# Forty weight columns instead of 64 in three groups of products, and PSUM pairs as three fixed tiles, in a chunked RWKV-7 kernel with a feed-forward block

## The chip, the cores and the metric

The kernel runs on one core of a Trainium2 chip. The core has five engines, each with its own queue of instructions: PE (matrix products; its weight loads are shown as PEld), DVE (vector work), ACT (activations and copies), POOL (vector work without access to PSUM) and SP (here it issues transfers). The metric is the device time of one execution in microseconds (us), lower is better; times are given as the median of several runs. All data are 32-bit floats. A matmul of this type that is no transpose shows as two weight loads and two matmul records in the profile, so the record counts below are twice the program's matmuls, except for transposes.

PSUM, where PE writes, has eight banks; a bank is 128 partitions by 512 floats.

## The reference

```python
# r, k, v, w, a, b: (batch 4, heads 8, time 768, D 40)
state = zeros((B, H, D, D))
for t in range(S):
    y[:, :, t] = einsum('bhd,bhde->bhe', rt, state)
    Sa = einsum('bhde,bhe->bhd', state, at)
    state_decay = state * wt[:, :, None, :] - einsum('bhd,bhe->bhde', Sa, bt)
    state = state_decay + einsum('bhd,bhe->bhde', vt, kt)

# x: y with (heads, D) as features, 3072 tokens x 320
h = x @ w_in                                   # 320 -> 2048
g = h * clip(h + 3.0, 0.0, 6.0) / 6.0
out = g @ w_out                                # 2048 -> 320
```

## The kernel before, in words

The recurrence is done in blocks of 64 time steps. A unit is one block of two batches with all eight heads; 24 units, four to a group of 128 steps (two blocks by two pairs of batches). For each unit, preparation stages (function `prepare`) load and transpose the inputs, form running products of the decays on DVE (scans, L541 and L552), and the score products; an inversion of a triangular matrix for a whole group runs on DVE as a long row of small steps (`invert`, L738 and L744), with its second half on PE (`third_block`, L773 and L796). The unit's own stages (function `step`) then follow: R (L853), U (L891), U-transpose (L911), the product with the state before the block (rS, L927), the new state (sn, L946, its addition on DVE at L954), scores (H, C, from `scores`, L509) and y (L969). ACT copies most of these results out of PSUM (U L895, U-transpose L917, rS L933, S L880, EV L692); POOL multiplies y by the decay and SP moves it into the layout of the feed-forward block.

The products of a block are small: D is 40, a block 64 steps. The kernel uses the PE array in quarters of 64 rows by 64 columns, and four matmuls, one to a quarter, work side by side. In y, U-transpose and rS the weights are slices of 64 columns (`SLOT`) although a head has 40; the other 24 columns produce rows of the result that nobody reads. The new state's products (L946) load 64 columns in the first four units and 40 (`D`) in the rest.

The feed-forward block works on 128 tokens, one unit, in two jobs of eight feature tiles each. A job has an `expand` (L1051: 24 matmuls, 48 records, into two banks called the hidden ones, half `c` = 0 and 1, 512 columns each) and a `contract` (L1092: eight matmuls, 16 records, into a bank called `o`). Between them, for each half in turn, ACT takes the relu out of the hidden bank (L1066) and DVE forms the product with the same bank (L1067) into `gt`. The function `results` issues them in the order relu 0, product 0, relu 1, product 1. The contract of one job is issued after the expand of the next. 48 jobs in all. Jobs are dealt out between the unit stages by `pieces`, a matmul group at a time.

The order of instructions on every engine is the order in which the Python code issues them. Semaphore waits come from a layer that follows who wrote and read each tile; two uses of one tile by different engines are put in order where they touch.

PSUM: one bank `one`, one bank `o`, and three pairs of banks. A call to `pair()` gives the next pair, of which the two banks hold what the two row halves of the array write. Before, two of the pairs are slots of a pool (`pair`, two buffers) and the third is in a pool of its own (`lent`). The three are called in turn. When the feed-forward block begins (`begun_ffn`), the `lent` pool is closed and a pool for two hidden banks takes its place; from then on `pair()` asks the pool with two slots. Such a pool gives a new tile the slot whose last use comes first in the order of issue, and a tile's first writer waits for every user of the slot's last tile.

Of the kernel before, what the change touches and what calls it, by code (L numbers as in the profile page):

```python
# [8 lines left out]
F32 = mybir.dt.float32  # L9
# [3 lines left out]
AF = mybir.ActivationFunctionType  # L13
AX = mybir.AxisListType
PSUM = bass.MemoryType.PSUM

P = 128
# [3 lines left out]
SLOT = 64  # L21
# [3 lines left out]
def _ap(ap, extra, dims):  # L25

    return bass.AP(tensor=ap.tensor, offset=ap.offset + extra, ap=[list(ap.ap[0])] + dims)
# [3 lines left out]
def kernel(  # L31
# [42 lines left out]
    nc = tc.nc  # L74
    B, H, T, D = r.shape
# [17 lines left out]
    ps = ctx.enter_context(tc.tile_pool(name="ps", bufs=1, space=PSUM))  # L93
# [3 lines left out]
        return ps.tile(shape, F32, name=tag, tag=tag, bufs=bufs)  # L97

    ring, open_half = deque(), [None]
    lent = tc.tile_pool(name="lent", bufs=1, space=PSUM)  # L100
    pools = {"lent": lent.__enter__(), "pair": ps}
    pairs = deque([("pair", 2), ("pair", 2), ("lent", 1)])

    def pair():

        pairs.rotate(-1)
        tag, bufs = pairs[-1]
        return pools[tag].tile([P, 2, 512], F32, name=tag, tag=tag, bufs=bufs)

    def begun_ffn():  # L110

        lent.__exit__(None, None, None)
        pairs.clear()
        pairs.append(("pair", 2))
        pools["h"] = ctx.enter_context(tc.tile_pool(name="hidden", bufs=1, space=PSUM))


    def ps_any(shape):
# [21 lines left out]
    def ps_pair(*dims):  # L140

        n = 1
        for d in dims:
            n *= d
        if shared[0] is None or shared[1] + n > 512:
            shared[:] = pair(), 0
            open_half[0] = None
        at = shared[1]
        shared[1] += n
        views, step = [], n  # L150
        for d in dims:
            step //= d
            views.append([step, d])
        t = shared[0][:]
        return [_ap(t, at, views), _ap(t, at + 512, views), _ap(t, at, [[512, 2]] + views)]
# [6 lines left out]
        out=ident[:], in_=ones, pattern=[[1, P]],  # L162
# [4 lines left out]
        out=ones[:, 0:BL], in_=ones[:, 0:BL], pattern=[[1, BL]],  # L167
# [3 lines left out]
        out=ones[BL:P, 0:BL], in_=ones[BL:P, BL:P], pattern=[[1, BL]],  # L171
# [5 lines left out]
    three = const.tile([P, 1], F32, name="three")  # L177
# [43 lines left out]
    for i in range(3):  # L221
        t = const.tile([P, H, BL], F32, name=f"score{i}")
# [7 lines left out]
    RR = const.tile([P, 2, NPR * D + SLOT - D], F32, name="RR")  # L230
# [6 lines left out]
    for p in range(NP):  # L237
        t = const.tile([P, 2, NPR, SLOT], F32, name=f"state{p}")
        nc.vector.memset(t[:], 0.0)
        state.append(t)  # L240
        t = const.tile([P, 2, NPR], F32, name=f"last{p}")
# [16 lines left out]
    for i, (x, y) in enumerate([(0, DFF // 2), (0, NJ // 2)]):  # L258
        for n, z in enumerate((x, y)):
            t = win[:, :, z:z + H * SLOT] if i == 0 else \  # L260
                wout[:, z:z + 4, :].rearrange("p j m -> p (j m)")[:, 0:2 * H * SLOT].rearrange(
                    "p (n x) -> p n x", n=2)
            t = t.rearrange("p n (h e) -> p n h e", e=SLOT)
            name = ("WA", "BK")[i][n]
# [3 lines left out]
    for u in range(2):  # L268
        t = win2[:, u * NPR * P:(u + 1) * NPR * P]
# [216 lines left out]
    def by_banks(x):  # L486
        return x[:].rearrange("p r (q t) -> p q r t", q=2)
# [8 lines left out]
    def turned(name):  # L496
        return tmp.tile([P, NPR, P], F32, name=name, tag="turned", bufs=5)

    def half(i, n=SLOT):
        return slice(SLOT * i, SLOT * i + n)  # L500
# [316 lines left out]
    def step(i):  # L817

        n, o = i % NU, data[i]
        g, p = names[i]  # L820
# [3 lines left out]
        m = {}  # L824
# [78 lines left out]
        def s_UT():  # L903

            up = ps_pair(2, P)
            for j in range(2):
                for s in range(2):
                    for x in range(2):
                        for rs in range(2):
                            pr = 2 * j + rs  # L910
                            nc.tensor.matmul(out=up[x][half(rs), j, half(x ^ s)],  # L911
                                             lhsT=RR[half(x), s, pr * D:pr * D + SLOT],
                                             rhs=tinv[half(x), n * H + 4 * s + pr, :],
                                             start=True, stop=True)
            yield PE
            m["UT"] = turned("UT")
            nc.scalar.activation(out=m["UT"][:].rearrange("p (x j) t -> p x j t", x=2), in_=up[2],  # L917
                                 func=AF.Copy, scale=-1.0)

        def s_rS():  # L920

            ysp = ps_pair(2, 2, BL)
            for j in range(2):
                for q in range(2):
                    for s in range(2):
                        for rs in range(2):
                            nc.tensor.matmul(out=ysp[rs][half(s), j, q, :],  # L927
                                             lhsT=m["S"][half(rs, D), q, j, half(s)],
                                             rhs=m["RT"][half(rs, D), 2 * s + j, half(q)],
                                             start=(j == 0 and q == 0), stop=(j == 1 and q == 1))  # L930
            yield PE
            ys = m["ys"] = tmp.tile([P, NPR, 2, BL], F32, name="ys", tag="yg", bufs=2)
            nc.scalar.activation(out=ys[:].rearrange("p (j r) q t -> p r j (q t)", r=2),  # L933
                                 in_=ysp[2].rearrange("p r j q t -> p r j (q t)"), func=AF.Copy)
# [26 lines left out]
        def s_y():  # L961
            y = ps_pair(NPR, BL)
            for name in "KB":
                for pr in range(NPR):
                    j, rs = pr // 2, pr % 2
                    for s in range(2):
                        for q in range(2):
                            h = 2 * pr + s
                            nc.tensor.matmul(  # L969
                                out=y[q][half(s), pr, :],  # L970
                                lhsT=o[name][half(q), h * D:h * D + SLOT],
                                rhs=m[name][half(q), 4 * rs + 2 * s + j, :],
                                start=(name == "K" and pr == 0), stop=(name == "B" and pr == NPR - 1))
            yield PE
            yg = m["yg"] = tmp.tile([P, NPR, P], F32, name="yg", tag="yg", bufs=2)
            if fresh:
                nc.vector.tensor_tensor(out=by_banks(yg), in0=y[2], in1=by_banks(o["G"]), op=ALU.mult)
                return
            x = m["ys"][:].rearrange("p r q t -> p q r t")
            nc.vector.tensor_tensor(out=x, in0=y[2], in1=x, op=ALU.add)  # L980
            nc.gpsimd.tensor_tensor(out=yg[:], in0=m["ys"][:].rearrange("p r q t -> p r (q t)"),  # L981
                                    in1=o["G"][:], op=ALU.mult)
# [27 lines left out]
    HJ, NQ = NJ // 2, 4  # L1010
# [33 lines left out]

    def expand(xt, j0, gts):

        hp = [pools["h"].tile([P, NQ, P], F32, name="h", tag="h", bufs=2) for _ in range(2)]
        begun = [0, 0]

        def add(c, i, lhsT, rhs):  # L1050
            nc.tensor.matmul(out=hp[c][:, i, :], lhsT=lhsT, rhs=rhs, start=(begun[c] == 0),  # L1051
                             stop=(begun[c] == 3 * NQ - 1))
            begun[c] += 1

        def short():
            narrow.clear()
            for i in range(NQ):
                for c in range(2):
                    add(c, i, win2[half(c), (j0 + i) * P:(j0 + i + 1) * P], xt[half(c), 2, :])
            if begun[0] + begun[1] == 6 * NQ:  # L1060
                results()

        def results():
            for c in range(2):
                gt = ffn.tile([P, NQ, P], F32, name="gt", bufs=5)
                nc.scalar.activation(out=gt[:], in_=hp[c][:], func=AF.Relu, bias=three[:], scale=1.0)  # L1066
                nc.vector.scalar_tensor_tensor(out=gt[:], in0=gt[:], scalar=6.0, in1=hp[c][:],  # L1067
                                               op0=ALU.min, op1=ALU.mult)
                gts.append(gt)

        narrow.append(short)
        for c in range(2):
            for t in range(2):
                for i in range(NQ):
                    j = c * HJ + j0 + i
                    add(c, i, win[:, t, j * P:(j + 1) * P], xt[:, t, :])
                if c == 1 and t == 1 and not narrow:
                    results()
                yield True
        if not spread[0] and narrow:  # L1080
            short()
            yield True
# [138 lines left out]
    n, cleared = 0, []  # L1221
    while not third:
        aside(1)
        if not third:
# [3 lines left out]
            if converted[0] >= 2 and not cleared:  # L1228
                cleared.append(True)
                for z in range(0, P, BL):  # L1230
                    nc.scalar.activation(out=tinv[z + L:z + BL, :, 0:L], func=AF.Copy, scale=0.0,
                                         in_=_ap(three[z + L:z + BL], 0, [[0, NH], [0, L]]))
# [157 lines left out]
    m = 0  # L1390
# [61 lines left out]
```

## Time and profile before

| what | value |
|---|---|
| runs (3) | median 799.31 us, 798.29 to 800.55 |
| profiled execution, span from first to last instruction | 798.4 us |
| h product L1051, PE | 2304 records, 251.3 us busy |
| output product L1092, PE | 768 records, 229.6 us busy |
| product with h, L1067, DVE | 96, 62.0 us busy, mean 681 ns |
| relu of h, L1066, ACT | 96, 62.2 us busy, mean 686 ns |
| y, L969, PE (into the tiles called pair) | 1472 records, 27.8 us busy |
| chain that ended last, by engine | PE 73%, DVE 13%, issue 5% |

The span agrees with the lowest run; the median is 0.9 us above it. Busy time counts a moment once, whichever and however many instructions of a group are at work. The chain that ended last is followed back from the last instruction to what released it. A line such as L1051 is the line of the kernel before; in the changed kernel the same lines stand five lower from L112 on.

### The profile page before, as it was taken

What the parts mean: (1) busy time and instruction counts of PE and PEld (TensorE: products, weight loads), DVE (VectorE), ACT (ScalarE), POOL (GpSimd) and SP (SyncE); (2) the same over time, 40 slices, a digit from 0 to 9 for tenths busy, and PEclk for the clock granted to TensorE, in tenths of its full rate; (3) what the DMA queues carried; (4) which work ended last, traced back from release to release, by engine and by line L of the source; (5) the groups of instructions that cost most, each with busy time, mean ns of one, the idle gap of its engine ahead of it and who ended that gap; (6) DMA issues with size and microseconds to landing.
All of it is one profiled execution on the core that took longest, in us unless ns stands there. A gap on an engine that the chain in (4) does not pass through costs nothing.

```text
span 798.4 us, 35294 instructions
## 1 busy us (share of the span) xinstructions
PE 727.1 (91%) x15832; PEld 617.9 (77%) x15832; DVE 501.3 (63%) x986; ACT 307.2 (38%) x648; POOL 176.3 (22%) x318
## 2 busy tenths in 40 slices
PE   5624676999999989999999999999999999999998
PEld 4624575878778878888888888888888888888886
DVE  8889787679555699455698445898444983322210
ACT  2336653321654424453344453324444324412111
POOL 6403012420322222223124123304122202000000
PEclk9855888999999999999999999999999999999999
DMA  9484563420224321233222233213222101110000
GB/s 122 88 183 111 143 169 56 76 50 9 49 52 68 64 51 31 50 64 56 44 43 43 44 59 64 46 33 58 44 51 46 24 17 30 30 25 13 14 19 17
DMA packets 174214, 45.02 MB, mean 56 GB/s; under 512 B 157424, under 2 KB 172784, under 8 KB 174064
## 3 DMA queue, kind: packets, MB, share of 16 engines
q1 hardware_dynamic: 169760, 42.03, 27.6%
q8 instruction: 125, 2.05, 1.1%
q10 hardware_dynamic: 4304, 0.74, 0.6%
q14 instruction: 25, 0.20, 0.1%
HBM read 34.08 MB, written 3.93 MB: 48 GB/s over the span
## 4 chain that ended last, share of the span: by engine, by line
PE 73%; DVE 13%; issue 5%; SPq 3%; DMA 3%; ACT 2%; POOL 1%; DVEq 0%; POOLq 0%; ACTq 0%
PE h L1051 25%; PE o L1092 22%; PE pair L509 4%; PE pair L969 3%; PE pair L946 2%; DVE prod L738 2%; DVE x L744 2%; PE pair L481 2%; PE one L471 2%; SPq L455 2%; PE pair L853 2%; PE pair L891 2%; DVE prods L541 1%; PE pair L927 1%; DVE wm L552 1%
## 5 line engine op out<-in xcount | busy, mean ns | idle before, releaser
L1051 PE MATMUL h<-xt,win 128*128 128x128 f32 (+1 forms) x2304 | 251.3, 283 | 2.7 <-DVE gt L1067 2.7
L1051 PEld LDWEIGHTS h<-xt,win 128*128 128x128 f32 (+1 forms) x2304 | 231.8, 193 | 19.8 <-issue 4.4
L1092 PE MATMUL o<-wout,gt 128*128 128x320 f32 x768 | 229.6, 442 | 0.0
L1092 PEld LDWEIGHTS o<-wout,gt 128*128 128x128 f32 x768 | 138.1, 190 | 50.4 <-issue 0.2
L1067 DVE SCALAR_TENSOR_TENSOR gt<-gt,h 128x512 f32<-128x512 f32 x96 | 62.0, 681 | 70.5 <-ACT gt L1066 70.5
L1066 ACT ACTIVATE gt<-h,three 128x512 f32<-128x512 f32 x96 | 62.2, 686 | 99.7 <-PE h L1051 99.3
L981 POOL TENSOR_TENSOR yg<-ys,gam 128x512 f32<-128x512 f32 x22 | 39.0, 1772 | 160.3 <-DVE ys L980 73.7
L738 DVE TENSOR_TENSOR prod<-x 128x30 f32<-128x30 f32 (+9 forms) x180 | 67.1, 373 | 8.8 <-POOL x L723 3.3
L660 POOL TENSOR_TENSOR KBt<-K,rgt 128x320 f32<-128x320 f32 x22 | 19.0, 865 | 212.6 <-ACT rgt L649 197.2
L744 DVE TENSOR_TENSOR x<-x,prod 128x30 f32<-128x30 f32 (+9 forms) x180 | 62.2, 345 | 5.4
L954 DVE TENSOR_TENSOR state<-pair,state 40x320 f32<-40x320 f32 (+1 forms) x44 | 21.4, 487 | 65.4 <-PE pair L946 39.1
L517 DVE COPY_PREDICATED score<-mask,pair 128x512 f32<-128x512 int32 x71 | 50.0, 723 | 1.0 <-PE pair L509 0.5
L980 DVE TENSOR_TENSOR ys<-pair,ys 128x512 f32<-128x512 f32 x22 | 15.2, 690 | 40.8 <-PE pair L687 21.8
L552 DVE TENSOR_TENSOR_SCAN wm<-wm,start 128x528 f32<-128x528 f32 x24 | 37.8, 1574 | 0.8
L541 DVE TENSOR_TENSOR_SCAN prods<-wm,start 128x528 f32<-128x528 f32 x24 | 30.8, 1288 | 10.1 <-ACT wm L538 10.0
L831 ACT ACTIVATE RT<-pair 128x512 f32<-128x512 f32 x21 | 12.5, 597 | 52.8 <-PE pair L481 52.8
L692 ACT ACTIVATE EV<-pair 64x320 f32<-64x320 f32 x44 | 19.0, 432 | 32.9 <-PE pair L687 22.3
L806 ACT ACTIVATE tinv<-pair 32x256 f32<-32x256 f32 x48 | 18.0, 375 | 30.8 <-PE pair L796 30.1
L569 POOL COPY gam<-prods 128x256 f32<-128x256 f32 x24 | 22.5, 938 | 31.4 <-DVE prods L541 30.6
L969 PE MATMUL pair<-score,KBt 64*64 64x64 f32 x1472 | 27.8, 224 | 1.2 <-DVE state L954 1.2
L1110 ACT ACTIVATE ob<-o 128x320 f32<-128x320 f32 x22 | 9.6, 435 | 49.0 <-PE o L1092 24.8
L969 PEld LDWEIGHTS pair<-score,KBt 64*64 64x64 f32 x1472 | 24.5, 137 | 3.8 <-DVE state L954 1.8
(262 smaller groups left out, 1049.0 us busy)
## 6 DMA issues: line engine op xcount, KB each, us to landing
V<-in_v_dram SPq DMA_DIRECT2D x96, 40.0 KB
out_dram<-ob SPq DMA_DIRECT2D x47, 80.0 KB
R<-in_r_dram SPq DMA_DIRECT2D x92, 40.0 KB
B<-in_b_dram SPq DMA_DIRECT2D x42, 80.0 KB
K<-in_k_dram SPq DMA_DIRECT2D x42, 80.0 KB
W<-in_w_dram SPq DMA_DIRECT2D x37, 80.0 KB
A<-in_a_dram SPq DMA_DIRECT2D x37, 80.0 KB
xt<-yg SPq DMA_DIRECT2D x72, 40.0 KB
```

The source lines that it names most:

```text
L509: nc.tensor.matmul(out=o[i][half(q), n, :], lhsT=lhs[half(i, D), n ^ (2 * q * swap), half(q)], rhs=rhs[half(i, D), n, half(q)], start=True ...
L517: nc.vector.copy_predicated(out=x[:].rearrange("p (i h) t -> p i h t", i=2), mask=mask8, data=o[2])
L541: nc.vector.tensor_tensor_scan(out=prods[:].rearrange("p r m i -> p (r m i)"), data0=wm[:, 0:SCAN], data1=start[:], initial=0.0, op0=ALU.m ...
L552: nc.vector.tensor_tensor_scan(out=back, data0=back, data1=start[:], initial=0.0, op0=ALU.mult, op1=ALU.add)
L738: nc.vector.tensor_tensor(out=pv, in0=_ap(x[:], (i + 1) * L + i, [[L, n], [0, i]]), in1=_ap(x[:], i * L, [[0, n], [1, i]]), op=ALU.mult,)
L744: nc.vector.tensor_tensor(out=rest, in0=rest, in1=pv, op=ALU.add)
L969: nc.tensor.matmul(out=y[q][half(s), pr, :], lhsT=o[name][half(q), h * D:h * D + SLOT], rhs=m[name][half(q), 4 * rs + 2 * s + j, :], start ...
L981: nc.gpsimd.tensor_tensor(out=yg[:], in0=m["ys"][:].rearrange("p r q t -> p r (q t)"), in1=o["G"][:], op=ALU.mult)
L1051: nc.tensor.matmul(out=hp[c][:, i, :], lhsT=lhsT, rhs=rhs, start=(begun[c] == 0), stop=(begun[c] == 3 * NQ - 1))
L1066: nc.scalar.activation(out=gt[:], in_=hp[c][:], func=AF.Relu, bias=three[:], scale=1.0)
L1067: nc.vector.scalar_tensor_tensor(out=gt[:], in0=gt[:], scalar=6.0, in1=hp[c][:], op0=ALU.min, op1=ALU.mult)
L1092: nc.tensor.matmul(out=op[:], lhsT=gts[c][:, n, :], rhs=wout[:, c * HJ + r * NQ + n, :], start=((split or r == 0) and c == 0 and n == 0), ...
```

## The change

In y (L969) and U-transpose (L911) the weight slices become 40 columns wide, and so do the state's slices in rS (L927); the results fill 40 instead of 64 partitions of each half. The two pools of pairs give way to three tiles that are allocated once. `pair()` hands them out in strict turn; when the feed-forward block begins, the tile whose turn is next leaves the round, and its two banks become the two hidden banks, for good: the tile is a single one for both halves.

In the built program every engine has the same instructions in the same order as before, apart from the widths and the waits. PE has 75 wait instructions fewer, ACT 24 and DVE 19 more. PE's waits for its own earlier matmuls go from 142 to 53. A relu (L1066) waits for the earlier product (L1067) of the same job or the job before in 63 cases of 96, where it was 12.

```diff
     ring, open_half = deque(), [None]
-    lent = tc.tile_pool(name="lent", bufs=1, space=PSUM)
-    pools = {"lent": lent.__enter__(), "pair": ps}
-    pairs = deque([("pair", 2), ("pair", 2), ("lent", 1)])
+    pairs = deque(ps.tile([P, 2, 512], F32, name=f"pair{i}") for i in range(3))
+    hidden = []
 
     def pair():
 
         pairs.rotate(-1)
-        tag, bufs = pairs[-1]
-        return pools[tag].tile([P, 2, 512], F32, name=tag, tag=tag, bufs=bufs)
+        return pairs[-1]
 
     def begun_ffn():
 
-        lent.__exit__(None, None, None)
-        pairs.clear()
-        pairs.append(("pair", 2))
-        pools["h"] = ctx.enter_context(tc.tile_pool(name="hidden", bufs=1, space=PSUM))
+        hidden.append(pairs.popleft())
...
-                            nc.tensor.matmul(out=up[x][half(rs), j, half(x ^ s)],
-                                             lhsT=RR[half(x), s, pr * D:pr * D + SLOT],
+                            nc.tensor.matmul(out=up[x][half(rs, D), j, half(x ^ s)],
+                                             lhsT=RR[half(x), s, pr * D:pr * D + D],
...
-                            nc.tensor.matmul(out=ysp[rs][half(s), j, q, :],
-                                             lhsT=m["S"][half(rs, D), q, j, half(s)],
+                            nc.tensor.matmul(out=ysp[rs][half(s, D), j, q, :],
+                                             lhsT=m["S"][half(rs, D), q, j, half(s, D)],
...
-                                out=y[q][half(s), pr, :],
-                                lhsT=o[name][half(q), h * D:h * D + SLOT],
+                                out=y[q][half(s, D), pr, :],
+                                lhsT=o[name][half(q), h * D:h * D + D],
...
-        hp = [pools["h"].tile([P, NQ, P], F32, name="h", tag="h", bufs=2) for _ in range(2)]
+        hp = [hidden[0][:, c].rearrange("p (n t) -> p n t", t=P) for c in range(2)]
...
-                nc.scalar.activation(out=gt[:], in_=hp[c][:], func=AF.Relu, bias=three[:], scale=1.0)
-                nc.vector.scalar_tensor_tensor(out=gt[:], in0=gt[:], scalar=6.0, in1=hp[c][:],
+                nc.scalar.activation(out=gt[:], in_=hp[c], func=AF.Relu, bias=three[:], scale=1.0)
+                nc.vector.scalar_tensor_tensor(out=gt[:], in0=gt[:], scalar=6.0, in1=hp[c],
                                                op0=ALU.min, op1=ALU.mult)
```

## The prediction

> **What bounds the kernel now.** I first read the busy times of the whole span, then the same by stretches of 100 us.
>
> ```profile
> PE 727.1 (91%) x15832; PEld 617.9 (77%) x15832; DVE 501.3 (63%) x986; ACT 307.2 (38%) x648; POOL 176.3 (22%) x318
> ```
>
> ```profile
> 200.00:300.00 100.00, 94.63 (x2351) 78.43 (x2351) 64.09 (x126) 44.87 (x104) 27.34 (x50) 1.00 0.32 57
> 300.00:400.00 100.00, 99.49 (x2352) 85.73 (x2351) 63.45 (x124) 42.41 (x98) 25.58 (x42) 1.00 0.27 49
> 400.00:500.00 100.00, 99.54 (x2303) 85.18 (x2303) 64.19 (x122) 44.32 (x99) 26.17 (x37) 1.00 0.27 51
> ```
>
> The columns after the length are PE, PEld, DVE, ACT, POOL, granted clock. From 200 us PE has 0.5 to 5 us of idle time in 100. It takes its work in a fixed order, so a microsecond saved on PE shortens the span, and a microsecond in which PE waits for something new lengthens it. DVE and ACT have room on average. The waits of PE come next: over the whole run the reuse of the hidden banks costs it little.
>
> ```profile
> PE h L1051 <- DVE gt L1067: 2.7, 4, 2.1
> ```
>
> How close that is, the timeline after one expand shows (start, length, engine, line).
>
> ```profile
> 252.02 1.27 ACT L1066 ACTIVATE gt<-h,three 128x512 f32<-128x512 f32 x2 [1.36 <-PE h L1051]
> 252.74 1.28 DVE L1067 SCALAR_TENSOR_TENSOR gt<-gt,h 128x512 f32<-128x512 f32 x2 [1.10 <-ACT gt L1066]
> 253.53 1.16 PE L1051 MATMUL h<-xt,win 128*128 128x128 f32 x8
> ```
>
> The two relus run back to back, and the second runs beside the first product. PE starts the next expand at 253.53, 0.10 us after the first product's end (252.74 + 0.69 = 253.43), while the second product still runs until 254.02.
>
> **The change: narrower loads.** Queues keep their order and no DMA moves. Of the 15832 matmul records, 768 (L911), 704 (L927) and 1536 (L969) load 40 columns instead of 64; all stream 64. Their rates are read off starts on PE's timeline.
>
> ```profile
> 297.46 0.68 PE L891 MATMUL pair<-RR,tinv 64*64 64x40 f32 x32
> 297.95 0.67 PE L911 MATMUL pair<-tinv,RR 64*64 64x64 f32 x32
> 298.44 0.65 PE L927 MATMUL pair<-RT,S 40*64 40x64 f32 x32
> 298.91 0.65 PE L620 MATMUL pair<-bt,at 40*64 40x64 f32 x32
> ```
>
> ```profile
> 299.49 2.42 PE L1092 MATMUL o<-wout,gt 128*128 128x320 f32 x8
> 301.74 4.83 PE L1051 MATMUL h<-xt,win 128*128 128x128 f32 x48
> ...
> 306.74 0.52 PE L946 MATMUL pair<-V,KBt 64*40 64x40 f32 x32
> 307.07 0.55 PE L946 MATMUL pair<-U,KBt 64*40 64x40 f32 x32
> ```
>
> ```profile
> 368.74 1.16 PE L969 MATMUL pair<-score,KBt 64*64 64x64 f32 x64
> 369.72 0.63 PE L687 MATMUL pair<-V,score 64*64 64x40 f32 x32
> ```
>
> Loads of 64 take 0.49/32 = 15.3 ns a record with 40 streamed columns (L891) and with 64 (L911), 14.7 in L927, 0.98/64 = 15.3 in L969. Load 40 with stream 40 (L946) takes 0.33/32 = 10.3. So a load of 64 sets a floor. Load 40 with stream 64 is in no row. One end: the load alone sets the pace, 10.3, a gain of 5.0 ns x 2304 + 4.4 x 704 = 14.6 us. Other end: no gain. In L1092 the stream of 320 columns takes 2.25/8 = 281 ns, 0.88 ns a column, so 64 columns take 56 ns on one quarter of the array and 14.1 a record with four quarters at work: 1.2 x 2304 + 0.6 x 704 = 3.2 us. This is the nearest row, since the stream stays; some overhead remains, and I take **-2.0**. A loss is excluded: no row of 40 columns is slower than its like of 64.
>
> [...]
>
> **Fewer waits of PE on itself.** The built program has 53 instead of 142. Between L946 and L509 the start gap is 80 ns with such a wait (12 times) and 25 without: 12 x 0.055 = **-0.7**. Elsewhere gaps with and without are alike (153 and 152 from L481 to L853), so nothing. ACT gets 24 and DVE 19 wait instructions more; such a one takes 51 ns where PE's load queue shows it, 2.2 us if all lay on the path, but they mostly repeat what PE's own wait has covered: 0, with 2.2 kept for the high end.
>
> **Hidden tile.** The two banks become one tile, and the built program orders its users by the tile: the first relu waits for both halves' matmuls, the second relu for the first product, the next expand's first matmul for the second product. First product's end to PE: 0.03 + 0.69 (relu) + 0.03 + 0.68 (product) + 0.05 = 1.48 us, where PE could start 0.05 after it. [...] I read for each of the 48 expands how long after the first product's end the next one began: 0.05 at 111.57 us, 1.06 at 194.63, 0.10 at 253.53, 0.05 at 284.34, 0.15 at 404.72 and 520.51, elsewhere over 2.0, where other matmuls hide it. Stalls: 1.43 + 0.42 + 1.38 + 1.43 + 1.33 + 1.33 = 7.3. The first falls ahead of a wait of 7 us for a weight DMA at 114.6 in the chain and goes: **+5.9**. The contract that reads these results comes an expand later, so it waits for nothing.
>
> **What queues behind the later relu.** ACT and DVE work in order.
>
> ```profile
> 128.71 1.27 ACT L1066 ACTIVATE gt<-h,three 128x512 f32<-128x512 f32 x2 [2.68 <-PE h L1051]
> ...
> 129.86 0.60 ACT L933 ACTIVATE ys<-pair 128x512 f32<-128x512 f32 x1
> ...
> 130.51 0.69 PE L509 MATMUL pair<-RT,UT 40*64 40x64 f32 x32 [0.30 <-ACT ys L933]
> ...
> 132.00 1.28 DVE L1067 SCALAR_TENSOR_TENSOR gt<-gt,h 128x512 f32<-128x512 f32 x2
> ```
>
> The second relu moves from 129.29 to 132.71, L933 and PE's L509 by the same **3.4**. At 264.2 PE waits for L917 behind a relu that moves 1.8, of which 0.55 was slack: 1.24. At 228.7 (EV, L692) 0.86. DVE is held 0.72 longer in every expand (relu and one hand-over between its two products); PE waits for what follows at 173.5 (score, 0.95) and 204.8 to 206 (state, then zs, 1.2). Together **+7.7**; ACT's copies at 373.9 and 489.7 (S, L880) also slip 2 to 3 us, but PE needs them blocks later.
>
> **Pairs in fixed turn.** The pool gave L853 and then L796 the same two banks, because the other pair still held B's transposes; fixed turn gives L796 the pair that L593 reads.
>
> ```profile
> 208.88 0.74 PE L796 MATMUL pair<-zs,tt 32*32 32x32 f32 x64 [0.44 <-DVE wm L582]
> 209.24 0.68 DVE L593 TENSOR_TENSOR bt<-pair,rgam 128x512 f32<-128x512 f32 x1
> ```
>
> L796 would start 0.05 after 209.92 instead of at 208.88: 1.10. The same reading at each new wait: 215.2 0.33, 293.2 1.14, 326.1 0.21, 352.9 1.09, 442.7 0.51, 468.7 1.09, 559.1 1.09, 585.9 0.53. Sum **+7.1**.
>
> **Both together.** At seven of these places (194.6, 284, 326, 404, 442, 520, 559) the awaited DVE result ends a stretch in which DVE had no pause, and one or two holds lie in it: 7 x 0.75 = 5.3 to 10.5; I take **+7**.
>
> **Sum**: 798.4 + 5.9 + 7.7 + 7.1 + 7 - 2.0 - 0.7 = 823.4 us. The median of the runs is 0.9 over the span: **824.3**, 824.
>
> **Rivals.**
> 1. *The new waits partly hide*: a PE that stalls once finds the next result ready, so only the two sums of PE's direct waits remain, 13.0: 799.3 + 13.0 - 2.7 = 810. For it: DVE is 63% busy. Against: the stalls lie tens of us apart.
> 2. *The load sets the pace*: -14.6 instead of -2.0 gives 811.7; since an earlier PE waits longer for DVE, about a third comes back, 816. For it: L946's 10.3. Against: L1092's stream.
> 3. *Faster than before*: the same 10.3 ns at L911, L927, L969, while the new waits are covered. 799.3 - 14.6 - 0.7 = 784. It decides only where the waits cost under 15.3 us; the 3.4 at 130.5 and the 7.1 of the pairs, with nothing else ready on PE, speak against.
> 4. *DVE becomes the bound* in the inversion stretches (270 to 300, 395 to 420, 510 to 535): two holds everywhere (10.5) and 5 us more from ACT's late copies: 799.3 + 20.7 + 10.5 + 5 - 2.7 = 833.
> That the change doesn't do what it says is excluded by its widths: 3008 records load 40.
>
> **How the numbers follow.** Forecast 64%, rival 1 12%, rival 2 12%, rival 4 7%, rival 3 3%, no change 2%. The likeliest's own range: low end 799.3 + 20.7 + 3 - 4, 819; high end 799.3 + 20.7 + 10.5 + 2.2 - 2.7, 830. The range takes in rivals 1 and 2 below and 4 above: 809 to 833. A measurement of this kernel tells 0.3% from no change: faster 0.03, same 0.02, slower 0.95.
>
> **What would show it.** The second relu starts at the first product's end, not beside it; PE's waits for DVE gt at L1051 grow from 2.7 to about 10 us; L796 waits for L593 six times; L969's start gap a record falls to 14 to 15 ns, not 10. PE's busy share falls. It would be wrong if the products' waits stay as they are or the three lines run at 10 ns.

## The result, and the profile after

The changed kernel takes 824.89 us (median of 5 runs, 824.28 to 829.72) where the kernel before took 799.31 on the same chip: slower by a factor of 1.0332, 95% interval 1.0308 to 1.0355. The forecast of 824 us falls on it. The profiled execution has a span of 823.2 us, 24.8 more than before.

The busy times of the profile after, and its chain of work that ended last:

```profile
PE 735.3 (89%) x15832; PEld 623.8 (76%) x15832; DVE 504.8 (61%) x986; ACT 309.8 (38%) x648; POOL 174.6 (21%) x318
...
PE 58%; DVE 26%; issue 6%; ACT 5%; DMA 2%; POOL 2%; SPq 1%; DVEq 0%; POOLq 0%; ACTq 0%
```

The engines do as many instructions in about as many busy microseconds as before; PE has 8.2 us more, part of it at half clock, as shown below. The chain shows where the time went: DVE's share rises from 13% to 26%, because PE now stands still until DVE is done. By stretches of 100 us (length; PE, PEld, DVE, ACT, POOL; granted clock; DMA share; GB/s):

```profile
200.00:300.00 100.00, 90.26 (x2102) 74.44 (x2101) 55.95 (x104) 41.58 (x96) 27.62 (x50) 0.97 0.29 51
300.00:400.00 100.00, 94.31 (x2292) 80.75 (x2292) 63.58 (x127) 40.60 (x90) 21.62 (x31) 0.98 0.25 47
400.00:500.00 100.00, 95.62 (x2160) 81.73 (x2161) 66.86 (x131) 41.76 (x94) 23.21 (x38) 1.00 0.24 45
```

From 300 to 500 us PE had 0.5 us of idle time in each 100; now it has 4 to 6. Two columns moved, not one: the granted clock, 1.00 in all three stretches before, is 0.97 and 0.98 in the first two. That second movement was not foreseen.

The waits of PE after 90 us (line that waited, engine and line it waited for; total, times, longest). Lines stand five lower than before: L1046 was L1051, L791 was L796, L504 was L509, L682 was L687.

```profile
PE pair L1046 <- DVE gt L1062: 11.0, 6, 3.5
PE pair L791 <- DVE bt L588: 8.6, 7, 1.6
PE pair L466 <- issue: 4.5, 1, 4.5
PE pair L504 <- ACT ys L928: 3.5, 1, 3.5
PE pair L682 <- DVE bt L588: 2.6, 1, 2.6
PE pair L682 <- DVE score L512: 2.5, 1, 2.5
```

The reuse of the hidden banks (first line) cost 2.7 us before. The list of before has no wait of L796 or L687 for `bt`, and 0.3 us of L509 for `ys`. The timeline around one expand shows the order that the single hidden tile forces (start, length, engine, line):

```profile
261.34 0.69 ACT L1061 ACTIVATE gt<-pair,three 128x512 f32<-128x512 f32 x1 [1.04 <-PE pair L1046]
...
262.06 0.69 DVE L1062 SCALAR_TENSOR_TENSOR gt<-gt,pair 128x512 f32<-128x512 f32 x1 [1.03 <-ACT gt L1061]
...
262.79 0.69 ACT L1061 ACTIVATE gt<-pair,three 128x512 f32<-128x512 f32 x1 [0.76 <-DVE gt L1062]
...
263.50 0.69 DVE L1062 SCALAR_TENSOR_TENSOR gt<-gt,pair 128x512 f32<-128x512 f32 x1 [0.75 <-ACT gt L1061]
...
264.25 0.38 PE L1046 MATMUL pair<-xt,win 128*128 128x128 f32 x1 [1.34 <-DVE gt L1062]
```

Relu, product, relu, product now run one after the other, each 0.02 to 0.04 us behind the last, on two engines that take turns. Before, ACT ran both relus in one stretch and PE went on after the first product; here PE starts 1.50 us after that product's end (262.75). And one of the new waits for a pair, which takes the tile that DVE is still reading:

```profile
215.56 0.67 DVE L588 TENSOR_TENSOR bt<-pair,rgam 128x512 f32<-128x512 f32 x1
216.29 0.64 PEld L791 LDWEIGHTS pair<-zs,tt 32*32 32x32 f32 x64 [2.10 <-DVE bt L588]
216.29 0.75 PE L791 MATMUL pair<-zs,tt 32*32 32x32 f32 x64 [1.59 <-DVE bt L588]
```

The n-th matmul record of both traces is the same product, so the lateness of the one against the other can be followed through the run. Each sudden rise is a new stall. Counted from 128 us (the start-up, where the two executions wait differently for their first inputs, leaves the changed kernel 0.4 us ahead), the lateness is made of:

| where (times of the kernel before, us) | us |
|---|---|
| expand waits for the second product: 194.6, 253.5, 284.3, 404.7, 520.5 | 7.1 |
| work behind the later relu and product: 130.5 (3.2, of which 1.7 is given back by 150), 173.5, 204.8, 206.0, 228.7, 264.2 | 5.2 |
| pairs in fixed turn: 208.9, 215.2, 293.2, 326.1, 352.9, 442.7, 468.7, 559.1, 585.9 | 9.3 |
| PE at half clock at 132 (1.8) and after 217, 265 and 309 us (4.7) of the changed run | 6.5 |
| one more wait at 578.4 (1.4), less three places where lateness is given back (1.5) | -0.1 |
| spread over all the rest, the narrower loads in it | -2.8 |
| sum (24.8 at the end, and the 0.4; the rows are rounded) | 25.2 |

The fourth row is seen in windows placed before and after two stalls:

```profile
212.00:216.00 4.00, 2.44 (x68) 1.70 (x68) 3.94 (x9) 1.25 (x3) 1.88 (x5) 1.00 0.42 72
216.00:222.00 6.00, 5.71 (x132) 5.43 (x136) 0.93 (x2) 1.50 (x4) 0.00 (x0) 0.72 0.12 30
258.00:264.00 6.00, 4.90 (x145) 4.13 (x143) 2.17 (x4) 3.35 (x7) 1.35 (x2) 1.00 0.27 46
264.00:270.00 6.00, 5.75 (x89) 5.36 (x90) 1.28 (x4) 2.44 (x7) 1.88 (x3) 0.72 0.24 41
270.00:276.00 6.00, 6.00 (x164) 5.28 (x164) 4.86 (x10) 1.35 (x3) 1.98 (x4) 1.00 0.33 64
```

Right after the stall at 216.3 (L791) and the one at 264.2 (L1046) the clock column reads 0.72 over 6 us: half speed for 3.4 us of them. Six microseconds later it is full again. While it lasts the lateness grows by 1.54, 1.58 and 1.62 us at the three places, 4.7 in all.

A longer spell begins within the wait for `ys` of 3.5 us that ends at 133.5. First the changed kernel, then the kernel before:

```profile
128.00:132.00 4.00, 2.05 (x102) 1.80 (x100) 3.85 (x10) 0.69 (x1) 2.19 (x6) 0.93 0.33 56
132.00:136.00 4.00, 2.48 (x35) 1.97 (x36) 2.08 (x4) 1.17 (x2) 0.00 (x0) 0.50 0.23 54
136.00:140.00 4.00, 4.00 (x72) 2.73 (x71) 0.73 (x2) 0.00 (x0) 0.00 (x0) 0.68 0.51 87
```

```profile
128.00:132.00 4.00, 3.70 (x141) 3.21 (x140) 3.85 (x10) 1.75 (x3) 2.62 (x7) 0.98 0.44 70
132.00:136.00 4.00, 2.75 (x70) 1.88 (x69) 3.05 (x7) 0.00 (x0) 0.00 (x0) 1.00 0.23 54
136.00:140.00 4.00, 4.00 (x26) 3.19 (x25) 1.30 (x3) 0.54 (x2) 0.00 (x0) 1.00 0.52 89
```

The granted clock is half for 6.8 us, from 131.8 to 138.6, where the kernel before runs at full clock from 128.1 on. PE stands still for the first 1.8 of them; in the others the lateness grows by 1.8 us, waits apart.

### The profile page after: what moved, and what is told of

The parts are those of the page before. It is cut to its first block, busy times and chain, and to the rows that moved or that the text cites. A ratio compares the mean times of both kernels' runs of the same rounds, so it can differ in the third digit from the quotient of the medians.

```text
span 823.2 us, 35262 instructions
## 1 busy us (share of the span) xinstructions
PE 735.3 (89%) x15832; PEld 623.8 (76%) x15832; DVE 504.8 (61%) x986; ACT 309.8 (38%) x648; POOL 174.6 (21%) x318
## 4 chain that ended last, share of the span: by engine, by line
PE 58%; DVE 26%; issue 6%; ACT 5%; DMA 2%; POOL 2%; SPq 1%; DVEq 0%; POOLq 0%; ACTq 0%
PE pair L1046 20%; PE o L1087 18%; DVE prod L733 4%; DVE x L739 4%; DVE gt L1062 3%; PE pair L504 3%; PE pair L964 3%; DVE wm L547 3%; DVE score L512 2%; DVE prods L536 2%; ACT gt L1061 2%; PE one L466 2%; PE pair L941 2%; PE pair L886 2%; PE pair L476 1%
## 5 line engine op out<-in xcount | busy, mean ns | idle before, releaser
L1046 PE MATMUL pair<-xt,win 128*128 128x128 f32 (+1 forms) x2304 | 255.3, 286 | 11.0 <-DVE gt L1062 11.0
L1046 PEld LDWEIGHTS pair<-xt,win 128*128 128x128 f32 (+1 forms) x2304 | 235.2, 195 | 28.7 <-DVE gt L1062 13.4
L1062 DVE SCALAR_TENSOR_TENSOR gt<-gt,pair 128x512 f32<-128x512 f32 x96 | 65.8, 685 | 107.6 <-ACT gt L1061 105.7
L1061 ACT ACTIVATE gt<-pair,three 128x512 f32<-128x512 f32 x96 | 66.0, 687 | 169.6 <-PE pair L1046 104.3
L687 ACT ACTIVATE EV<-pair 64x320 f32<-64x320 f32 x48 | 20.7, 432 | 34.7 <-PE pair L682 25.7
L964 PE MATMUL pair<-score,KBt 64*40 64x64 f32 x1536 | 29.7, 233 | 0.0
L964 PEld LDWEIGHTS pair<-score,KBt 64*40 64x40 f32 x1536 | 25.9, 124 | 2.9 <-issue 1.1
L852 DVE TENSOR_TENSOR RR<-pair,EV 128x320 f32<-128x320 f32 x22 | 10.7, 487 | 25.4 <-PE pair L504 25.3
```

Of the source, the lines that this page charges most:

```text
L964: nc.tensor.matmul(out=y[q][half(s, D), pr, :], lhsT=o[name][half(q), h * D:h * D + D], rhs=m[name][half(q), 4 * rs + 2 * s + j, :], start ...
L1061: nc.scalar.activation(out=gt[:], in_=hp[c], func=AF.Relu, bias=three[:], scale=1.0)
```

## The experiments

The theory behind the forecast: the time goes to the two new orders, that of the hidden tile and that of the pairs, and the narrow loads give 2 us back. The rivals in the first five runs are that the narrow loads are worth 15 us (the load sets their pace) or that one of the two orders costs nothing alone. Times are medians; the kernel before is measured beside each group on the same chip.

**e1, the narrow loads without the new orders.** The results of a 40-column load fill 40 of each 64 partitions, while the readers read all 128. With fresh tiles from a pool, nothing in the program would write the other partitions. So the three fixed tiles stay, but are handed out in the order in which the pool gave its slots: 14 of the calls to `pair()` after the feed-forward block begins get the tile of the call before. The hidden banks are two pool tiles again, and the third pair is filled with zeros once (one DVE instruction more). Against the changed kernel:

```diff
+    calls = [0]
+    SAME = {85, 88, 120, 130, 140, 149, 157, 166, 176, 185, 193, 202, 212, 221}
...
-        pairs.rotate(-1)
+        calls[0] += 1
+        if calls[0] - 1 not in SAME:
+            pairs.rotate(-1)
         return pairs[-1]
...
-        hp = [hidden[0][:, c].rearrange("p (n t) -> p n t", t=P) for c in range(2)]
+        hp = [pools["h"].tile([P, NQ, P], F32, name="h", tag="h", bufs=2) for _ in range(2)]
```

> Three fixed pair tiles, handed out in the order in which the pools of the kernel before gave their slots, the two hidden banks as two tiles again, and the 40-column loads: the waits of before with the new widths. The forecast's theory (the new waits cost the time, the 64 streamed columns set the pace of the three products): 2.0 to 3.2 us less PE work, so 796 to 797.5 us, and 13 to 14.1 ns a record in the three groups. Rival, the load sets the pace: 10.3 ns a record, 785 us. Rival, fixed tiles or narrow loads cost something by themselves: over 800 us.

Measured: 795.05 us (12 runs, 792.72 to 797.65) beside 798.34 for the kernel before (17 runs); ratio 0.9954, interval 0.9939 to 0.9969. The gain is 3.3 us, about 1 more than expected and the size that the stream of 64 columns allows (3.2 in the prediction's second bound), not 14.6. This version is faster than both kernels, so the loss isn't in the narrow loads at all. Its busy times and chain, which stay close to those of the kernel before:

```profile
PE 729.4 (92%) x15832; PEld 618.8 (78%) x15832; DVE 501.7 (63%) x987; ACT 306.3 (39%) x648; POOL 176.5 (22%) x318
...
PE 75%; DVE 9%; issue 6%; DMA 4%; SPq 3%; ACT 2%; POOL 1%; DVEq 0%; POOLq 0%; ACTq 0%
```

**e2, the strict turn added.** e1 with the strict turn and without e1's filling with zeros; the hidden banks are still two tiles.

```diff
-        calls[0] += 1
-        if calls[0] - 1 not in SAME:
-            pairs.rotate(-1)
+        pairs.rotate(-1)
         return pairs[-1]
```

> As the run with the widths alone, but the pairs in strict turn; the hidden banks stay two tiles. The forecast's theory: the pairs' term alone, 7.1 us and little more, so 803 to 805 us, with six waits of L796 for L593's product. Rival, all of the loss comes from the hidden tile and a changed turn of the pairs is covered by other work: 796 to 798 us.

Measured: 806.07 us (805.07 to 807.57), ratio 1.0097, interval 1.0075 to 1.0119: 11.0 over e1, and 1 us over the upper end of what was expected. The waits of PE after 90 us (here L797 is the changed kernel's L791, L688 its L682, L1052 its L1046):

```profile
PE pair L797 <- DVE bt L594: 6.8, 7, 1.5
...
PE h L1052 <- DVE gt L1068: 2.8, 4, 2.1
PE pair L688 <- DVE bt L594: 2.6, 1, 2.6
```

The waits for `bt` are there, seven at L797 where six were expected, and the hidden banks' wait is the 2.8 of old: the two orders are separate mechanisms. Counted from 128 us, e2 falls 10.2 us behind e1. The rises at the pairs' nine places sum to 8.1; the rest is almost all half clock, three windows in e2 (4.6) against two in e1, at 131 and 172 us (2.7).

**e3, one hidden tile alone.** The kernel before, its pairs and its 64 columns, with the two hidden banks as one tile.

```diff
         pools["h"] = ctx.enter_context(tc.tile_pool(name="hidden", bufs=1, space=PSUM))
+        hidden.append(pools["h"].tile([P, 2, 512], F32, name="hid"))
...
-        hp = [pools["h"].tile([P, NQ, P], F32, name="h", tag="h", bufs=2) for _ in range(2)]
+        hp = [hidden[0][:, c].rearrange("p (n t) -> p n t", t=P) for c in range(2)]
```

> The kernel before, in which only the two hidden banks become one tile; pairs in their pools, loads of 64 columns. The forecast's theory: late second half on PE 5.9, queues behind the later relu 7.7, and the part of the 7 us of both together that falls on hidden places, 5 to 7: 818 to 820 us. Rival, only PE's direct wait for the second product counts and the queues behind the relu are covered: 805 to 807 us. [...]

Measured: 813.91 us (813.19 to 816.14), ratio 1.0198, interval 1.0175 to 1.0221: 15.6 over the kernel before, 4 to 6 under what was expected.

```profile
PE hid L1054 <- DVE gt L1070: 10.8, 6, 3.5
PE pair L512 <- ACT ys L936: 4.1, 1, 4.1
```

Both waits are about as large as in the changed kernel. What is less is the rest: of the stall at 130.5 us, 1.4 is given back by 146, the places at 173.5 and 228.7 lose less than was worked out for them, and after 136 us there is no half-clock window. Of the 5 to 7 charged for the two together (a wait that also holds a later result of DVE back), the prediction's seven places show 1.9 (0.9 at 194.6, 0.6 at 326.1, 0.3 at 442.7).

**e4, the changed kernel with loads of 64.** Both new orders, and y, U-transpose and rS as wide as before.

```diff
-                                lhsT=o[name][half(q), h * D:h * D + D],
+                                lhsT=o[name][half(q), h * D:h * D + SLOT],
```

(and likewise at U-transpose and rS)

> The changed kernel with loads of 64 columns again. The forecast's theory: 1.5 to 2.6 us slower than the changed kernel, some of the saved PE time being given back where PE waits for DVE, so 826 to 827.5 us. Rival, the load sets the pace: 835 us or more. Rival, the narrow loads are part of the loss: under 824 us.

Measured: 826.85 us (825.17 to 829.13), ratio 1.0365, interval 1.0338 to 1.0392. The narrow loads are worth 2.0 us within the changed kernel by the medians, 2.6 by the ratios. The two intervals overlap, so this is a middle value with some 2 us on either side; counted from 128 us, the lateness of the two profiled executions differs by 2.9.

**e5, both relus ahead of both products.** The changed kernel, with only the order of the four instructions of `results` changed.

```diff
-            for c in range(2):
-                gt = ffn.tile([P, NQ, P], F32, name="gt", bufs=5)
+            made = [ffn.tile([P, NQ, P], F32, name="gt", bufs=5) for _ in range(2)]
+            for c, gt in enumerate(made):
                 nc.scalar.activation(out=gt[:], in_=hp[c], func=AF.Relu, bias=three[:], scale=1.0)
+            for c, gt in enumerate(made):
                 nc.vector.scalar_tensor_tensor(out=gt[:], in0=gt[:], scalar=6.0, in1=hp[c],
```

> The changed kernel, in which both relus of a job are issued before both products. The hidden banks stay one tile, so PE still waits for the second product, but the second relu no longer waits for the first product: ACT is not held by a late DVE, and DVE is not held by a relu between its two products. The forecast's theory (queues behind the later relu, and DVE's longer hold, make up over half of the loss): 809 to 813 us. Rival, the loss is PE's own wait for the second half: 820 us or more, as that wait shrinks by 0.1 us at most where relu and product follow at once.

Measured: 814.51 us (812.14 to 815.85), ratio 1.0186, interval 1.0153 to 1.0218, beside 798.50: 1.5 over the range expected, and well under the rival's 820. Its waits of PE, with the same lines as the changed kernel but for the product, one lower:

```profile
PE pair L791 <- DVE bt L588: 8.6, 7, 2.0
PE pair L1046 <- DVE gt L1063: 6.6, 5, 3.2
```

The relu no longer stands behind a product on another engine. The wait for the hidden tile falls from 11.0 to 6.6, that of L504 for `ys` from 3.5 to 0.4, and the pairs' wait stays at 8.6. The changed kernel's 824.89 less 814.51 is 10.4 (11.7 by the ratios, each beside its own kernel before): this much of the loss comes from the alternation of ACT and DVE, and an order of issue takes it away without a second tile.

**e6, what sets the pace of a narrow load.** e1 with y's stream cut to 40 columns: 24 of each 64 time steps of y aren't computed.

```diff
-                                out=y[q][half(s, D), pr, :],
+                                out=y[q][half(s, D), pr, 0:D],
...
-                                rhs=m[name][half(q), 4 * rs + 2 * s + j, :],
+                                rhs=m[name][half(q), 4 * rs + 2 * s + j, 0:D],
```

> As the run with the widths alone, but y's products stream 40 columns instead of 64, so 24 of the 64 time steps of each block's y are left out. The forecast's theory (with a load of 40 the stream sets the pace): y's records go from about 14 to 10 ns, 1536 x 4 ns = 6 us of PE work less, 790 to 792 us. Rival, a floor of another kind holds y's records at 14 ns whatever the stream: 796 to 797.5 us, as the run with the widths alone.

Measured: 791.93 us (791.24 to 792.93), ratio 0.9904, interval 0.9872 to 0.9935, beside 798.50. One group of y and the next instruction on PE's timeline, first in the changed kernel, then in e6 (start, length, line, count of records):

```profile
386.85 1.10 PE L964 MATMUL pair<-score,KBt 64*40 64x64 f32 x64
387.78 0.63 PE L682 MATMUL pair<-V,score 64*64 64x40 f32 x32
```

```profile
363.60 0.83 PE L975 MATMUL pair<-score,KBt 64*40 64x40 f32 x64
364.24 0.66 PE L693 MATMUL pair<-V,score 64*64 64x40 f32 x32
```

0.93/64 = 14.5 ns a record with 64 streamed columns, 0.64/64 = 10.0 with 40. The load has 40 columns in both. The stream is what held the narrow loads back. The time lies in the expected range, but the saving doesn't arrive whole: 1536 records at 4.5 ns less are 6.9 us of PE work, and e6 is only 3.1 us below e1 by the medians, 4.0 by the ratios. New waits of PE take up a part of it; they were not followed further.

**e7 and e8, is PE's stall what halves the clock?** After six runs, the half-clock windows were the part of the loss without an experiment. e7 is e2 with five products of the identity matrix put into an idle bank ahead of four L797 at which PE had stood 1.2 to 1.6 us; e8 is e2 again, on the same chip.

```diff
+        tps[0] += 1
+        if tps[0] - 1 in (2, 5, 7, 8):
+            fill = bank("one", [P, 512], 1)
+            for _ in range(5):
+                nc.tensor.matmul(out=fill[:, 0:P], lhsT=ident[:], rhs=ident[:], start=True, stop=True)
```

> The kernel of the strict turn (e2_fixed_turn, 806.07 us), with five products of the identity matrix with itself (20 records of 32 to 128 columns each, some 1.1 us by the rows of this size) put into the idle bank ahead of the third, sixth, eighth and ninth group's L797, where PE stood idle 1.55, 1.42, 1.43 and 1.17 us for DVE. They compute nothing that is read. Theory (a stall that leaves PE idle long enough makes the clock gate grant half speed for 3.4 us, which happened at 206.7, 353.4 and 472.9 us and cost about 1.7 us each): with PE at work the granted clock stays full at these three places, the fillers lie inside the stalls, and the time falls by 3 to 5 us, to 801 to 803. Rival (the half clock has another cause, and the fillers only add work): the windows of half clock stay, and the time is 806 to 810.

> The strict turn again, on the same chip as the run with the fillers, for a direct comparison: 805 to 807.5 us by every theory. If the half-clock windows follow from the stalls, they are again at 206.7, 353.4 and 472.9 us of this program, within a microsecond; if the chip throttles at random, they lie elsewhere.

Measured: 804.75 us with the fillers (6 runs, 804.52 to 806.74; ratio 1.0073, interval 1.0055 to 1.0090) and 805.06 without (6 runs, 804.74 to 808.05; ratio 1.0082, interval 1.0063 to 1.0101), beside 799.10. The gain of 3 to 5 us isn't there: the run with the fillers lies between the ranges of its theory and of its rival, and within 0.3 us of the repeat, which is where it was expected. Both expectations of where the windows lie failed. In the run with the fillers:

```profile
206.00:210.00 4.00, 3.88 (x85) 3.33 (x86) 2.31 (x5) 1.17 (x3) 0.00 (x0) 1.00 0.54 104
...
213.00:216.00 3.00, 1.46 (x72) 1.24 (x63) 0.00 (x0) 1.72 (x5) 0.92 (x2) 1.00 0.02 5
216.00:220.00 4.00, 4.00 (x96) 3.78 (x98) 0.00 (x0) 1.85 (x6) 0.76 (x1) 0.59 0.30 50
```

and in the repeat without them:

```profile
204.00:206.50 2.50, 1.01 (x67) 0.97 (x68) 1.43 (x4) 0.62 (x2) 0.00 (x0) 1.00 0.61 120
206.50:210.00 3.50, 3.50 (x98) 3.27 (x100) 0.69 (x1) 1.57 (x5) 0.00 (x0) 1.00 0.07 17
...
288.00:291.00 3.00, 0.36 (x10) 0.22 (x12) 2.96 (x8) 0.00 (x0) 0.00 (x0) 0.86 0.11 30
291.00:296.00 5.00, 5.00 (x45) 4.14 (x42) 4.72 (x12) 2.24 (x4) 0.00 (x0) 0.50 0.03 7
```

The fillers show as ten records and 1.3 us at each place, not the twenty expected. The filled places kept the full clock (206 to 210 in the first fence), and PE's waits for `bt` at that line fell from 6.8 to 1.9 us. But three other stalls, which no filler covered (at 171, 215 and 295 us), were followed by half clock in that run. In the repeat the stall of 1.5 us at 206, after which e2 had lost its clock, was followed by full clock (1.00), and the longer one at 288 to 291 by half. So the same program loses its clock at different stalls in different runs. No run shows that taking a stall away takes a window away: in e7 their number stayed three, and the repeat without fillers had two places (one of them two windows long).

What the traces of all runs have in common is this. Cut into stretches of 3.4 us from the clock's own changes, every drop after 135 us (19, in eight of the ten profiled executions; the kernel before and e3 have none) follows a stretch in which PE was busy for 23% to 61% of it, with one stall of 1.3 to 2.6 us; none follows a fuller one. Some stretches of 51% to 59% had no drop. Every drop seen there thus comes after a stall; which of the stalls is taken, and by what, stays open.

**The parts against the whole.** By medians: narrow loads -3.3 (e1), strict turn +11.0 (e2 less e1), one hidden tile +15.6 (e3), together +23.3, where the changed kernel has 824.89 - 799.31 = 25.6. What the parts cost only in company is 2.3, no more than the intervals leave open. Counted from 128 us in the profiled executions the parts are -1.1, +10.2 and +15.4, 24.5 against 25.2: 0.7. Either way it is small.

## Why the prediction was right, point by point

The direction, the size and the two new orders as its cause held, and the span came out 0.2 us from the working's sum (823.2 against 823.4). That closeness is luck: two terms were 6.4 us too large together, and 6.5 us that no term named made up for them. A smaller miss is the step from the span to the time of a run, put at 0.9 us: for the profiled execution of the changed kernel it is 1.7 (824.89 against 823.2), so that of the kernel before was hardly its lowest run.

- **Hidden tile, +5.9.** Right, with the chain of 1.48 us measured as 1.50. The sixth stall, at 111.6 us, appeared (1.44) and was given back in the wait of L471 that ends at 124 (1.52), as worked out.
- **Behind the later relu, +7.7.** The places are right, the sum is 5.2. At 130.5 PE waits 3.5 where it waited 0.3, so it loses 3.2 instead of 3.4, and half of that comes back within 20 us: the next steps of PE had waits before (1.2 us of L969 for the state, the largest) and have none now.
- **Pairs in fixed turn, +7.1.** The nine places and the prices are right but for 326.1 and 442.7, where DVE was later than in the profile of before; with these two it is 9.3. The prediction had put that lateness into the next term. It speaks of six waits of L796 for L593; its own list holds seven, and seven came.
- **Both together, +7: the term that failed.** Of the seven places only three cost more than their direct wait: 194.6 by 0.87, 326.1 by 0.98, 442.7 by 0.84; the other four by 0.05 to 0.14. That is 3.1, under the low end of 5.3 that the prediction gave. At the four the hold seems to have been absorbed ahead of the awaited result; no run isolates this. The parts against the whole point the same way: 0.7 to 2.3.
- **In its place, 6.5 us of half clock,** which no step named. The kernel before had such windows in its start-up, but none between 128 and 796 us in its profile, so none there gave a price. With 3.1 for 7, 5.2 for 7.7 and this 6.5, the sum is 823.5, 0.3 over the span.
- **Narrower loads, -2.0.** Right in kind: the stream sets the pace. From the first start to the last of a group, as the median over all groups, L964 runs at 14.1 ns a record instead of 15.0, U-transpose at 13.6 instead of 14.7, rS at 13.3 instead of 13.8: 0.9 x 1536 + 1.1 x 768 + 0.5 x 704 = 2.6 us; the runs give 2.0 (e4) and 3.3 (e1). Rivals 2 and 3 rested on 10.3 ns and fall with this; e6 shows that it takes a stream of 40 as well.
- **Fewer waits of PE on itself, -0.7, and the added wait instructions, 0.** The first is smaller: at the twelve places between L946 and L509, the 40 records around the step take 501 ns from start to start in the changed kernel and took 515 before, 12 x 0.014 = 0.2 us. The second is told apart by no run; what is left over in the table (-2.8, with the loads' 2.6 and this 0.2 in it) leaves nothing for it.
- **Rival 1** (the waits partly hide, 810) falls: PE's waits for `gt` went from 2.7 to 11.0 and the pairs' waits came on top, 8.6 in seven places. **Rival 4** (DVE the bound, 833): DVE's busy share fell to 61%, and the compounding cost 3.1 us, where this rival needed 10.5 and 5 more.

## What to carry to other kernels

Which tiles are one and which are two is part of the schedule: joining two banks into one tile, with not an instruction moved, cost 15.6 us here, and handing three tiles out in strict turn instead of the one freed first cost 11.0. When a new allocation makes a small saving possible, take the saving and keep the old order of reuse (e1: 795.05 us). And price a narrower weight load by what its record still streams, not by the load: with 40 columns loaded in both, a record of y took 14.5 ns with 64 streamed and 10.0 with 40 (e6).

## What was not expected of the hardware

A stall of PE of 1.3 to 2.6 us can be paid for twice. After some of them the granted clock is half for 3.4 us, which cost 1.5 to 1.6 us each in the changed kernel; with the longer spell at 132 us, half clock makes up 6.5 of the 25.2 counted from 128 us. From one run of the same program to the next the spells fall partly on other stalls (e2 at 207, 353 and 473 us, its repeat at about 290 to 297 and at 355, the stall that e2 has at 353), so a profile shows what they cost, not where they will be next time. In the stretch of 3.4 us ahead of each drop after 135 us PE was at work for 23% to 61% of the time: 54%, 61% and 23% ahead of the three in the changed kernel.
